# One written order for every engine, from the first load to the last store

## The chip, the cores and the metric

The kernel runs on one core of a Trainium2 chip. The metric is the device time of one execution in microseconds; smaller is better. The engines are named as in the profile: PE (TensorE, matmuls and transposes), DVE (VectorE), ACT (ScalarE), POOL (GpSimd) and SP (SyncE, which issues most DMAs). Each engine runs its own instructions strictly in the order of its queue. An instruction whose data are not there holds up everything behind it on the same engine.

## The reference

What is computed, cut to what matters (float32 in and out):

```python
# q, k, v: (4 batches, 8 heads, 768 tokens, 64)
gamma = 1.0 - 2.0 ** (-5.0 - np.arange(H))
for t in range(S):                       # retention, a state of 64 x 64 per head
    state = gamma * state + einsum('bhd,bhe->bhde', k[:, :, t], v[:, :, t])
    y[:, :, t] = 1/sqrt(D) * einsum('bhd,bhde->bhe', q[:, :, t], state)
x = y, heads side by side                # (4, 768, 512)
u = x + real(fft(fft(x, axis=1), axis=2))
un = (u - mean(u)) / sqrt(var(u) + 1e-6)
out = u + maximum(un @ w_ch1, 0) @ w_ch2     # 512 -> 2048 -> 512
```

## The kernel before, in words

**Work per batch.** A batch passes through five stages. In the attention stage the eight heads go in four pairs, numbered 0 to 3. Each pair has one load of q, one of k and one of v of 384 KB, casts to float16, transposes of q and k, scores (`wkA`) with a mask (`atm`), the chunk states (matmul `wkK`, decay into `s`) and the output (`wkY`, from the scores and from the states), which is scaled into `x`. The folding stage uses the symmetry of the transforms (`xab`, `eo`, `g`). The mixing stage makes the two transforms as matmuls (`ps`, `pq`), adds the residual (`u`) and normalizes it (`bst`, `un`). Then `un` is transposed to `unT`, by PE or by a DMA on SP. The MLP has a first product (`psh`, then relu into `ht`) and a second (`psc`, then `ob` and the store). The last batch uses seven products on sums of blocks in place of eight for its MLP (`hsum`, `wsum`). The MLP is most of PE's work, and the other stages of batch b+1 are woven into the MLP of batch b.

**What sets the order.** In the first batch, up to its first MLP matmuls, the order is written out: the strings FIRST and SECOND name one unit of work after another, and after each unit `pin()` chains the new instructions of every engine to the last one of the same engine, so that the scheduler cannot move them. The twelve loads of the first batch and the eight maskp constants are issued outside of these strings. The rest comes from `emit`: the units of a batch are put into streams, each with a first and a last due time as a fraction of a batch (DM0, TS0, DA0, LD0, MIX3, WS and others), all units are sorted by due time, and the Tile scheduler gives the order from there. `emit` pins POOL alone during batch 0 and every engine during the last batch; between them the scheduler is free. A unit there often has instructions of several engines: `a_unit`, for one, holds the score matmuls on PE and the mask product on DVE, and `ch_unit` the second product on PE, the addition on DVE and the store on SP.

**Names that the text uses.** A unit's name has its kind and then its pair or block. In the first batch `v30` and `v31` are the two halves of the cast of pair 3's v (on POOL and on ACT, L194 and L193), `v20` the cast of pair 2's v on ACT, `kv3` the state products of pair 3 (L516), `sc3` the scan behind them (L525), `am30` and `am31` score products, `yi20`, `yi21` and `yx2` the output products of pair 2 (L538, L548), `stx01` a small transpose, `x20`, `x21`, `x30`, `x31` the scaling into x (L193), `co4` a cosine table on ACT (L367), `s1m1` a part of the first transform (L782). `h00` to `h23` are the first MLP products of the first batch (L1135), `h00` the first of them and `h13` the one that the loads of batch 1 wait for. `w10` to `w13` and `w20` to `w23` are the loads of quarters of the two weights (L1311, L1318), 512 KB each, issued by POOL on a queue of its own, while all other loads go through SP.

In before POOL issues the weights in the order w10 w11 w12, v30's cast, w13, w20 to w23. The loads of batch 1 wait for the seventh weight and for `h13`:

```python
for x in (w_dma[after].ins, lb[0]["mm"].ins):
    tc.add_manual_dep(dma.ins, x.name, ...)      # after = 6
```

Of the kernel before, what the change touches and what calls it, by code (L numbers as in the profile page):

```python
# [11 lines left out]
AF = mybir.ActivationFunctionType  # L12
# [6 lines left out]
P = 128  # L19
# [13 lines left out]
DM0, DM1 = (0.120, 0.208, 0.265, 0.344), (0.004, 0.137, 0.232, 0.341)  # L33
TS0 = (0.249, 0.368, 0.406, 0.410, 0.479, 0.544, 0.680, 0.685)
TS1 = (-0.040, -0.020, 0.048, 0.585)
DA0, DA1 = (0.068, 0.080, 0.173, 0.203, 0.292, 0.326), (0.063, 0.067, 0.063, 0.158, 0.168, 0.189)
LD0, LD1 = (0.172, 0.226), (-0.370, 0.140)
HT0 = (0.655, 0.675, 0.673, 0.628)
NPE = 2
LOADS = "q0 k0 v0 q1 k1 v1 q2 k2 q3 k3 v2 v3"  # L40
# [9 lines left out]
FIRST = """  # L50
par qz0 hid hid5 gk3 q0 nid0 ta0 gk1 ta1 gk0 tq0 nid1 gk2 tn0 k00 eq0 tb0 si0 k01 v00 tk0 tn1 ab0
ek00 tb1 co0 ta3 q1 am01 tn3 ab1 am00 tb3 si1 ae000 si3 ta2 ab3 ae010 kv0 co1 ae011 yi00 tn2 sc0
co3 tb2 ab2 tq1 ae001 k10 si2 eq1 k11 co2 nsp tk1 ek10 yi01 v10 yx0 q2 am10 x01 kv1 ae100 am11 x00
sc1 tq2 k20 k21 q3 ae111 eq2 tk2 ae110 tq3 ek20 k30 ae101 am20 am21 ae200 w10 ae201 k31 ae211 yi10
yi11 ae210 yx1 tk3 w11 x10 ek30 eq3 ek31 ta4 w12 tn4 x11 am30 v30 tb4 am31 v20 ae300 stx01 fs0a
w13 si4 f512 kv2 fs0b ab4 yi20 ae301 yi21 co4 cdh0 sc2 v31 s1s10 w20 ae310 yx2 kv3 ae311 x20 s1s00
w21 sc3 x21 yi30 w22 fla yi31 yx3 flb cdh1 x31 w23 fd0 x30 xn1 f512 s1m0 fhb xn0 xm1 stx3 px1 fha
gc00a g0a fd1 s1s11 qe1 xm0 gr0 s1s01 xm2 s1m1 gc11b gc01a xmb gc11a stg00 xe gc01b gc10a stx4 gr3
stg01 g0b gr2 s21 g0c stg10 mu1 qn1 mu2 s22 ul1 stg11 qn2 uu1 stx2 ul2 ste1 gr1 un1 ste0 uu2 xl2
s23 qz1 s20 xu2 qn3 s25 ul3 qn0  # L60
"""
EARLY = (1,)
SECOND = """
h00 un2 ul0 xl3 uu0 xl0 ut1 uu3 h01 xu0 qn5 uu5 s24 xu3 ul5 h10 qn4 un3 xu5 h11 ul4 xl5 uu4 xl4
h12 xu4 ut2 h03 un4 h13 h22 h21 h23 h20 h02
"""
MIX3 = ((0.005, 0.085, 0.110, 0.125, 0.150), (0.190, 0.290, 0.310, 0.325, 0.350),
        (0.345, 0.415, 0.435, 0.460, 0.500))
WS = (0.6, 0.97)
H3_ACT = (0, 1, 2, 3, 5, 6, 7)  # L70
PROD = ((1, 4, 5, 2, 6, 7, 3), (1, 4, 6, 7, 5, 2, 3))
HS_AT = {3: (0, 4), 7: (4, 8)}
# [4 lines left out]
def kernel(  # L77
# [76 lines left out]
    def behind():  # L154
        for x in tc.nc.cur_bb.bb.instructions[mark[0]:]:
            if str(x.engine) in base:
                tc.add_manual_dep(x, base[str(x.engine)],
                                  mybir.DependencyInfo(mybir.DependencyClass.NoSync,
                                                       mybir.DependencyReason.DATA),
                                  reason="behind the first batch")  # L160

    def held(unit):
        def run():
            ins = tc.nc.cur_bb.bb.instructions
            n0 = len(ins)
            unit()
            for n in range(n0, len(ins)):
                m = n - 1
                while m >= 0 and ins[m].engine != ins[n].engine:
                    m -= 1  # L170
                if m >= 0:
                    tc.add_manual_dep(ins[n], ins[m].name,
                                      mybir.DependencyInfo(mybir.DependencyClass.NoSync,
                                                           mybir.DependencyReason.DATA),
                                      reason="casts in turn")
        return run

# [23 lines left out]
    def load_unit(b, i, after=None, names="qkv"):  # L201
        def run():
            h0 = 2 * PAIR_ORDER[i]
            for name in names:
                src = srcs[name]
                t = inp.tile([P, 2, NCH, D], f32, tag="in32", name=f"{name}32")
                rows = "h (p c) d -> p h c d" if b < NPE and name == "q" else \
                    "h (c p) d -> p h c d"
                dma = nc.sync.dma_start(t, src[b, h0:h0 + 2].rearrange(rows, p=P))
                if after is not None:  # L210
                    for x in (w_dma[after].ins, lb[0]["mm"].ins):
                        tc.add_manual_dep(dma.ins, x.name,
                                          mybir.DependencyInfo(mybir.DependencyClass.Sync,
                                                               mybir.DependencyReason.DATA),
                                          reason="loads in turn")
                if b > 1:
                    tc.add_manual_dep(dma.ins, a_of[b - 1, 1].ins.name,
                                      mybir.DependencyInfo(mybir.DependencyClass.Sync,
                                                           mybir.DependencyReason.DATA),
                                      reason="loads behind the transposes")  # L220
                in_of[name, b, i] = t
        return run

    for n in LOADS.split():
        load_unit(0, int(n[1]), names=n[0])()
# [59 lines left out]
    def late_consts():  # L285
        with tc.issue_after(lb[0]["una"].ins):
            for h in range(H):
                nc.scalar.activation(maskp[:, h // 2, h % 2], maskf, AF.Copy, bias=0.0,
                                     scale=float(gam[h] ** (-P)))
# [17 lines left out]
    def pad_unit():  # L307
        for j in range(2):
            nc.vector.memset(qzs[j][:, 0, :, D:P], 0.0)
            nc.vector.memset(qzs[j][:, 1, :, 0:D], 0.0)  # L310

    def qt_zeros():
        for j in range(2):
            nc.vector.memset(qts[j][0:D, 1], 0.0)
            nc.vector.memset(qts[j][D:P, 0], 0.0)
# [85 lines left out]
    def cast_unit(b, i):  # L401
        def run():
            h0 = 2 * PAIR_ORDER[i]
            q32, k32, v32 = (in_of.pop((n, b, i)) for n in "qkv")
            kd = kp.tile([P, NCH, 2, D], f16, tag="kd16", name="kd16")
            v16 = vp.tile([P, NCH, 2, D], f16, tag="v16", name="v16")
            with ExitStack() as es:
                if b < NPE:
                    if (b, i - 1) in last_cast:
                        es.enter_context(tc.issue_after(last_cast[b, i - 1].ins))  # L410
                    q16 = qzs[i % 2].rearrange("p h c d -> p (h c d)")[
                        :, 0:NCH * P].rearrange("p (c h d) -> p c h d", c=NCH, h=2)
                    es.enter_context(tc.issue_after(nc.gpsimd.tensor_scalar(
                        out=q16, in0=q32.rearrange("p h c d -> p c h d"), scalar1=1.0,
                        scalar2=1.0, op0=ALU.mult, op1=ALU.mult).ins))
                else:
                    q16 = qzs[i % 2]
                    for h2 in range(2):
                        dst = q16[:, h2, :, D * h2:D * h2 + D]
                        nc.gpsimd.tensor_scalar(out=dst, in0=q32[:, h2], scalar1=1.0,  # L420
                                                scalar2=1.0, op0=ALU.mult, op1=ALU.mult)
                for h2 in range(2):
                    kc = nc.gpsimd.tensor_scalar(out=kd[:, :, h2, :], in0=k32[:, h2],  # L423
                                                 scalar1=gkd[:, h0 + h2:h0 + h2 + 1],
                                                 scalar2=1.0, op0=ALU.mult, op1=ALU.mult)
                    if b < NPE:
                        es.enter_context(tc.issue_after(kc.ins))
                last_cast[b, i] = nc.gpsimd.tensor_scalar(
                    out=v16, in0=v32.rearrange("p h c d -> p c h d"), scalar1=1.0, scalar2=1.0,
                    op0=ALU.mult, op1=ALU.mult)  # L430
            q16_of[b, i], kd_of[b, i], v16_of[b, i] = q16, kd, v16
        return run
# [26 lines left out]
    def t0_unit(i, part):  # L459
        def run():  # L460
            if (0, i) not in at:
                at[0, i] = dict(kT=tp.tile([P, NCH, P], f16, tag="kT", name="kT"),
                                qT=qts[i % 2][:, 0])
# [6 lines left out]

    def te_unit(i, part, n=0):
        def run():
            st = at[0, i]
            tq = st["tq", part]
            if part == 0:
                scaled(on[f"eq{i}"], st["qT"].rearrange("p c t -> p (c t)").rearrange(
# [1052 lines left out]
```

## Time and profile before

| | us |
|---|---|
| median of 3 runs (lowest, highest) | 242.58 (242.52, 244.07) |
| the profiled execution: its span, first to last instruction | 240.1 |
| PE busy | 231.2 |
| DVE busy | 189.3 |
| ACT busy | 122.2 |
| POOL busy | 89.9 |

The median of the runs is 2.4 us above the span of the profiled execution; no other time of that execution is shown. Spans on the timeline count from the start of the profiled execution. A row of the timeline has the start, the length, the engine, the line, the operation, output and inputs with their shapes, how many instructions the row joins, and in brackets how long the engine sat idle before it and what ended that. PEld is TensorE's loading of weights, SPq the issuing of a DMA by SyncE. In the rows of DMA queues, q1 is the queue of SP's loads, stores and transposes, q0 that of POOL's weights.

### The profile page before, as it was taken

How to read it: one execution, taken by the hardware profiler on the slowest of the kernel's cores; microseconds unless marked ns; L12 is line 12 of the kernel's file. 1: busy time of each engine (PE TensorE's matmuls, PEld its weight loads, DVE VectorE, ACT ScalarE, POOL GpSimd, SP SyncE). 2: the span in 40 equal slices, each digit the busy share in tenths (PEclk: the TensorE clock that was granted, in tenths of full speed). 3: DMA queues.
4: the chain of work that ended last, by engine and by line, in shares of the span. 5: the costliest groups of instructions: out<-in, count | busy, mean ns of one | idle time of the engine just before them, and what ended most of it. 6: DMA issues, size and time to landing. Idle time of an engine off the chain costs nothing.

```text
span 240.1 us, 5658 instructions
## 1 busy us (share of the span) xinstructions
PE 231.2 (96%) x2161; PEld 159.3 (66%) x2161; DVE 189.3 (79%) x484; ACT 122.2 (51%) x273; POOL 89.9 (37%) x149
## 2 busy tenths in 40 slices
PE   6888899999999999999999999999999999999995
PEld 2465799765765645665567546665567458898884
DVE  7869989877897788996886778899985856777274
ACT  6777775667956345741247423741247316253330
POOL 6667746264400068690000554680000502240302
PEclk9659999999999999999999999999999999999999
DMA  8999999999899647999999558787100141131202
GB/s 175 252 267 195 207 197 201 230 274 248 217 220 215 120 109 164 210 189 144 263 271 212 108 110 227 131 110 171 64 26 0 26 131 44 25 111 25 87 3 87
DMA packets 99466, 36.41 MB, mean 152 GB/s; under 512 B 89840, under 2 KB 96624, under 8 KB 99440
## 3 DMA queue, kind: packets, MB, share of 16 engines
q1 hardware_dynamic: 95072, 31.79, 63.4%
q0 software_dynamic: 4224, 4.19, 10.8%
q8 instruction: 17, 0.28, 0.5%
q14 instruction: 9, 0.07, 0.1%
q10 hardware_dynamic: 144, 0.07, 0.1%
HBM read 27.26 MB, written 6.29 MB: 140 GB/s over the span
## 4 chain that ended last, share of the span: by engine, by line
PE 80%; DVE 6%; ACT 5%; POOL 3%; DMA 2%; issue 2%; SPq 0%; ACTq 0%; POOLq 0%
PE psc L1157 22%; PE psh L1118 19%; PE psh L1199 9%; PE psc L1270 8%; PE psh L1135 4%; PE wkA L622 3%; PE ps L760 3%; PE wkY L676 2%; DMA k<-in_k_dram 2%; PE wkY L672 1%; PE pq L952 1%; ACT qTz L584 1%; PE wkK L641 1%; PE pq L1006 1%; PE tq L468 1%
## 5 line engine op out<-in xcount | busy, mean ns | idle before, releaser
L1157 PE MATMUL psc<-w,ht 128*128 128x512 f16 x288 | 68.5, 379 | 0.0
L1118 PE MATMUL psh<-unT,w 128*128 128x384 f16 x320 | 59.5, 326 | 0.0
L989 POOL TENSOR_TENSOR u<-u,x 128x256 f32<-128x256 f32 x18 | 11.6, 645 | 99.2 <-DVE u L959 98.0
L1157 PEld LDWEIGHTS <-ht 128*128 128x128 f16 x288 | 27.3, 98 | 26.1 <-issue 0.2
L1118 PEld LDWEIGHTS <-w 128*128 128x128 f16 x320 | 29.9, 98 | 16.0 <-issue 0.6
L1122 ACT ACTIVATE ht<-psh 128x384 f16<-128x384 f32 x46 | 22.3, 489 | 23.9 <-PE psh L1118 23.8
L625 DVE TENSOR_TENSOR atm<-wkA,maskp 128x512 f16<-128x512 f32 x36 | 23.9, 685 | 0.7 <-PE wkA L622 0.7
L1199 PE MATMUL psh<-unT,w 128*128 128x256 f16 x192 | 21.5, 272 | 0.0
L1124 DVE TENSOR_SCALAR ht<-psh 128x384 f16<-128x384 f32 x34 | 18.7, 550 | 2.1 <-PE psh L1118 2.0
L1199 PEld LDWEIGHTS <-w 128*128 128x128 f16 x192 | 18.7, 98 | 2.2
L1055 DVE BATCH_NORM_STATS2 bst<-u 128x6 f32<-128x512 f32 x21 | 14.5, 691 | 6.9 <-POOL u L991 6.8
L1204 ACT ACTIVATE ht<-psh 128x512 f16<-128x512 f32 x21 | 12.5, 597 | 12.9 <-PE psh L1199 7.9
L1161 DVE SCALAR_TENSOR_TENSOR ob<-psc,stats,u 128x512 f32<-128x512 f32 x18 | 13.4, 745 | 6.9 <-PE psc L1157 6.7
L651 DVE SCALAR_TENSOR_TENSOR s<-s,gk,wkK 128x128 f16<-128x128 f16 x48 | 16.3, 339 | 1.9 <-ACT s L647 1.3
L684 ACT ACTIVATE x<-wkY,gexp 128x384 f16<-128x384 f32 x24 | 12.8, 581 | 9.7 <-PE wkY L676 9.7
L1060 ACT ACTIVATE un<-u,stats 128x512 f16<-128x512 f32 x15 | 10.8, 720 | 10.7 <-DVE stats L1056 7.7
L423 POOL TENSOR_SCALAR kd<-k,gexp 128x384 f16<-128x384 f32 x24 | 13.9, 588 | 3.1 <-DMA k<-in_k_dram 3.1
L622 PE MATMUL wkA<-qTz,kT 128*128 128x256 f16 x72 | 13.5, 272 | 0.2
L991 POOL TENSOR_TENSOR u<-u,x 128x256 f32<-128x256 f32 x18 | 11.4, 635 | 2.7 <-DVE stats L1056 1.8
L1135 PE MATMUL psh<-unT,w 128*128 128x128 f16 x192 | 11.4, 219 | 0.0
L954 ACT COPY qn<-pq 128x128 f32<-128x128 f32 x18 | 4.9, 274 | 12.4 <-PE pq L952 12.3
L622 PEld LDWEIGHTS <-kT 128*128 128x128 f16 x72 | 6.8, 98 | 6.3 <-ACT kT L589 0.4
(220 smaller groups left out, 432.0 us busy)
## 6 DMA issues: line engine op xcount, KB each, us to landing
q<-in_q_dram SPq DMA_DIRECT2D x16, 384.0 KB, 6.2
k<-in_k_dram SPq DMA_DIRECT2D x16, 384.0 KB, 5.5
v<-in_v_dram SPq DMA_DIRECT2D x16, 384.0 KB, 6.4
out_dram<-ob SPq DMA_DIRECT2D x18, 256.0 KB, 2.8
w<-in_moe_w_ch_dram POOLq DMA_DIRECT2D x8, 512.0 KB, 10.5
out_dram<-o SPq DMA_DIRECT2D x2, 512.0 KB, 2.9
out_dram<-o SPq DMA_DIRECT2D x3, 128.0 KB, 1.7
unT<-un SPq DMA_TRANSPOSE x15, 2.5
```

The source lines that it names most:

```text
L423: kc = nc.gpsimd.tensor_scalar(out=kd[:, :, h2, :], in0=k32[:, h2], scalar1=gkd[:, h0 + h2:h0 + h2 + 1], scalar2=1.0, op0=ALU.mult, op1=AL ...
L622: mm = nc.tensor.matmul(wk[:, c2], st["kT"][:, c, :], st["qT"][:, :, c, :], start=True, stop=True)
L625: nc.vector.tensor_tensor(out=st["atm"][:, 2 * part:2 * part + 2], in0=wk, in1=maskp[:, PAIR_ORDER[i]].unsqueeze(1).to_broadcast([P, 2, 2, ...
L651: nc.vector.scalar_tensor_tensor(out=s16[:, c], in0=s16[:, c - 1], scalar=gk2[:, hp:hp + 1], in1=wk[:, c - c0], op0=ALU.mult, op1=ALU.add)
L1055: nc.vector.bn_stats(bst, u[:, kb, :])
L1118: nc.tensor.matmul(psh, w116[:, cb, fb * P:(fb + 1) * P], unT[:, cb, rt * 384:(rt + 1) * 384], start=(cb == 0), stop=(cb == 3))
L1122: nc.scalar.activation(ht16[:, fb, :], psh, AF.Relu, bias=0.0, scale=-1.0)
L1124: nc.vector.tensor_scalar(out=ht16[:, fb, :], in0=psh, scalar1=-1.0, scalar2=0.0, op0=ALU.mult, op1=ALU.max)
L1135: mm = nc.tensor.matmul(psh[:, f], w116[:, cb, fb * P:(fb + 1) * P], unT[:, cb, kb * P:(kb + 1) * P], start=(cb == 0), stop=(cb == 3))
L1157: nc.tensor.matmul(psc, ht16[:, fb, rb3 * P:(rb3 + 1) * P], w216[:, fb, :], start=(fb == 0), stop=(fb == NFB - 1))
L1199: nc.tensor.matmul(psh[:, t], w116[:, cb, fb * P:(fb + 1) * P], unT[:, cb, p * 256:(p + 1) * 256], start=(cb == 0), stop=(cb == 3))
L1270: nc.tensor.matmul(ps[:, c0:c1], lh(f), rh(f)[:, c0:c1], start=first and f == 0, stop=last and f == 7, skip_group_check=True)
```

## The change

All units are split until each has instructions of one engine only: `t_unit` becomes `t_piece` (PE) and `te_piece` (ACT), `a_unit` becomes `a_piece` (PE) and `ma_piece` (DVE), `ch_unit` becomes `c_piece`, `o_piece` and `o_store`, `cast_unit` four `cast_piece`, and so on. One string ORDER of some 1,100 names then lists every piece of the kernel from the first load to the last store, and `play` runs the pieces in that order and pins every engine, SP with them, after each. A number ahead of a name is its batch (none for batch 0): `1kv0_0` is the first half of the state products of batch 1's pair 0, `1tk2` the transposes of batch 1's k of pair 2, `1ck0_0` and `1ck1_0` casts of k on POOL, `1cq_3` that of q of pair 3, `1lq3` its load, `1ut5` the DMA transpose of block 5 of un, `1h1_6` a first MLP product, `3dq3` and `3dk3` DMA transposes of q and k, `3a2_3` score products. The streams, the due times, `emit` and `held` are gone. The number of instructions of each operation is the same. The first batch's load order goes from q0 k0 v0 q1 k1 v1 q2 k2 q3 k3 v2 v3 to q0 k0 v0 k1 q1 k2 q2 v1 q3 k3 v2 v3. The weights are issued as w10 and w13 right behind the cast of v1, w11 ahead of v30, then w22, w12, w20, w21, w23.

The core of the diff:

```diff
-DM0, DM1 = (0.120, 0.208, 0.265, 0.344), (0.004, 0.137, 0.232, 0.341)
...
-LOADS = "q0 k0 v0 q1 k1 v1 q2 k2 q3 k3 v2 v3"
...
-FIRST = """
...
-sc1 tq2 k20 k21 q3 ae111 eq2 tk2 ae110 tq3 ek20 k30 ae101 am20 am21 ae200 w10 ae201 k31 ae211 yi10
-yi11 ae210 yx1 tk3 w11 x10 ek30 eq3 ek31 ta4 w12 tn4 x11 am30 v30 tb4 am31 v20 ae300 stx01 fs0a
-w13 si4 f512 kv2 fs0b ab4 yi20 ae301 yi21 co4 cdh0 sc2 v31 s1s10 w20 ae310 yx2 kv3 ae311 x20 s1s00
-w21 sc3 x21 yi30 w22 fla yi31 yx3 flb cdh1 x31 w23 fd0 x30 xn1 f512 s1m0 fhb xn0 xm1 stx3 px1 fha
...
+ORDER = """
+ta0 gk0 gk3 lq0 mp3 q0 par ta1 lk0 k00 mp1 nid0 f512 tn1 f512 gk2 tb1 si1 ab1 tn0 tb0 si0 qtz00
...
+qz0 k31 v10 ae111 ae101 mp7 kv1 lv2 yi11 sc1 am20 lv3 ae200 yi10 w10 yx1 x11 am21 w13 ae201 ae210
+q3 tq3 k30 eq3 v20 ae211 x10 tk3 ta4 ek31 v31 tn4 ek30 am31 ae310 tb4 ab4 si4 kv2 ae311 am30 w11
+v30 kv3 stx01 sc2 yi20 yi21 yx2 x20 x21 co4 ae301 yi31 w22 ae300 yi30 sc3 yx3 fs0a cdh0 fs0b s1s10
+fla flb x30 x31 xm1 g0a s1s00 fd0 fha w12 xm0 fhb fd1 xn1 g0b s1m0 s1s01 gc00a xmb xn0 s1s11 gc11b
+s1m1 g0c close gc01a mp6 w20 gr0 gc01b cdh1 gc11a gr3 w21 stx3 stg00 stx4 stg01 gc10a px1 s21
...
+h00 xu2 qn0 uu0 h01 ut1 te1 qn3 uu3 s25 ul3 h02 w23 h03 qn5 ul5 uu5 h13 1lv0 1lq0 1lk0 h11 xl2 ul0
+un2 ut2 te2 h12 qn4 uu4 ul4 xu0 mp0 h10 h23 xl0 h22 1lv1 1lq1 bn1 0p0_1 bn0 bn2 0rt0 h21 0p0_0
+1lk3 xl5 xu5 bn5 half un5 mp2 1lk1 xl3 0p1_1 xu3 bn3 1cv_0 h20 0p1_0 1ck1_0 1ck0_0 1kv0_0 1s0_0
...
-    def a_unit(b, i, part):
...
+    def a_piece(b, i, part):
         def run():
-            st = at[b, i]
-            if part == 0:
-                st["atm"] = ap_.tile([P, NCH, 2, P], f16, tag="atm", name="atm")
-            wk = ps_g.tile([P, 2, 2, P], f32, tag="g", name="wkA")
+            st = st_of(b, i)
+            wk = st["wk", part] = ps_g.tile([P, 2, 2, P], f32, tag="g", name="wkA")
             for c2 in range(2):
                 c = 2 * part + c2
                 mm = nc.tensor.matmul(wk[:, c2], st["kT"][:, c, :], st["qT"][:, :, c, :],
                                       start=True, stop=True)
-            a_of[b, i] = mm
+            if part == 2:
+                a_of[b, i] = mm
+        return run
+
+    def ma_piece(b, i, part):
+        def run():
+            st = st_of(b, i)
+            if "atm" not in st:
+                st["atm"] = ap_.tile([P, NCH, 2, P], f16, tag="atm", name="atm")
             nc.vector.tensor_tensor(
-                out=st["atm"][:, 2 * part:2 * part + 2], in0=wk,
+                out=st["atm"][:, 2 * part:2 * part + 2], in0=st["wk", part],
...
+            dma = nc.sync.dma_start(t, srcs[name][b, h0:h0 + 2].rearrange(rows, p=P))
+            if b == 1:
+                sync(dma, w_dma[6], lb[0]["mm"])
+            elif b > 1:
+                sync(dma, a_of[b - 1, 1])
...
-    def emit(streams):
...
+    def play(names):
+        for name in names:
+            units[name]()
+            pin()
+
+    units = first_units()
     pin()
...
-    emit(streams)
+    play(ORDER.split())
```

1057 lines of the change are left out of this document (497 added, 560 removed).

## The prediction

> **What bounds the kernel now.** I read the page's head and slices first, then the chain that ended last, then the busy time of three stretches.
>
> ```profile
> span 240.1 us, 5658 instructions
> ...
> PE 231.2 (96%) x2161; PEld 159.3 (66%) x2161; DVE 189.3 (79%) x484; ACT 122.2 (51%) x273; POOL 89.9 (37%) x149
> ...
> PE   6888899999999999999999999999999999999995
> ...
> PE 80%; DVE 6%; ACT 5%; POOL 3%; DMA 2%; issue 2%; SPq 0%; ACTq 0%; POOLq 0%
> ```
>
> The span is 240.1 us and the median of the runs 242.58, so 2.4 us lie outside the span; I make the sum inside it and add the result to 242.58. TensorE fills every slice but the first five and the last one, and 80% of the chain is TensorE.
>
> ```profile
> 0.00:33.60 33.60, 28.74 (x334) 19.97 (x335) 27.72 (x89) 25.12 (x56) 21.86 (x42) 0.85 1.16 217
> 33.60:237.40 203.80, 202.41 (x1829) 139.28 (x1826) 161.38 (x396) 97.11 (x218) 68.07 (x108) 1.00 0.69 141
> 237.40:240.20 2.80, 0.00 (x0) 0.00 (x0) 0.25 (x1) 0.00 (x0) 0.00 (x0) 0.89 0.36 115
> ```
>
> (Columns: stretch, its length, busy PE, PEld, DVE, ACT and POOL, granted clock, DMA share, GB/s.) The front, up to the first MLP matmul (unit h00), has a DMA share over 1 and no engine full. The middle is TensorE at full clock. The end is 2.8 us of last additions and stores.
>
> "Busy 202.41" hides small losses, since a matmul's end is modelled. Long pieces of the chain give the interval between matmuls when nothing is missing:
>
> ```profile
> 39.13 6.25 PE psh L1135 x112
> 134.19 10.36 PE psc L1157 x48
> 184.46 1.30 PE psh L1118 x8
> 197.47 6.99 PE psh L1199 x64
> ```
>
> That is 56 ns at 128 columns, 216 at 512, 163 at 384, 109 at 256. Both orders have the same matmuls from h00 on: 288x216 + 320x163 + 420x109 + 436x56, and 363 small ones that I put by their widths at 14.4 us (an estimate), together 198.9 us. Before needs 203.7, so the order's faults after h00 cost **4.8 us**. That is the most that a better order can win there. They show as many short waits, few of them large:
>
> ```profile
> 54.70 0.49 PE L578 MATMUL tq<-ident,kd 128*128 128x128 f16 x6 [0.25 <-ACT qTz L584]
> ```
> ```profile
> PE wkK L641 <- POOL v L428: 0.4, 1, 0.4
> PE ps L895 <- DVE xg L886: 0.2, 1, 0.2
> ```
>
> **The change, part by part.** No operation goes or comes; every engine's queue gets another order.
>
> *The front.* The loads go out in nearly the same order, v2 and v3 still last. The stretch from the last load to h00 now:
>
> ```profile
> 21.19 0.85 ACT L193 ACTIVATE v<-v 128x768 f16<-128x768 f32 x1
> 22.55 0.56 POOL L194 TENSOR_SCALAR v<-v 128x384 f16<-128x384 f32 x1 [1.50 <-DMA v<-in_v_dram]
> 22.62 0.51 ACT L367 ACTIVATE cd<-tmp,hpi 128x257 f16<-128x257 f32 x1
> 23.04 0.51 ACT L193 ACTIVATE v<-v 128x384 f16<-128x384 f32 x1
> 24.45 0.47 PE L516 MATMUL wkK<-v,kd 128*64 128x64 f16 x10
> 25.92 0.53 PE L548 MATMUL wkY<-s,qTz 64*128 64x64 f16 x10
> 26.49 1.05 ACT L193 ACTIVATE x<-wkY,gexp 128x384 f16<-128x384 f32 x2 [0.89 <-PE wkY L548]
> 27.57 0.63 ACT L741 ACTIVATE junk<-x 128x514 f16<-128x514 f16 x1
> 29.48 0.69 PE L782 MATMUL ps<-ssp,eo 128*128 128x193 f16 x6
> 33.61 1.06 PE L1135 MATMUL psh<-unT,w 128*128 128x128 f16 x16
> ```
>
> The written order puts kv3, which needs the last load, ahead of yi20, yi21 and yx2 of the pair before, and on ScalarE x10 between v20 and v31. Worked through: v20 to 22.04, x10 to 22.63, v31 to 23.15, kv3 to 23.65, then about 1.15 us of TensorE for stx01, yi20, yi21 and yx2 to 24.8; x20 and x21 (1.05) to 25.95, co4 (0.51, the row at 22.62) to 26.5, yi3 and yx3 to 27.0, x30 and x31 to 28.05, where before has 27.54. Then two "junk" means of 0.63 stand ahead of the first g copy, where before has one, and s1m1 waits for the bank that this copy frees: 0.25 more. h00 comes at 34.35 instead of 33.61: **+0.75**. Bounds: 0, if the chain closes up, and +2, if ScalarE, which also gets three maskp pieces early on, reaches v20 late (by its rows' sum it has 0.8 us to spare).
>
> *Weights ahead of loads.* POOL issues w10 and w13 right after the cast of v1, near 16 us by the sum of POOL's rows, and w11 ahead of v30; before, the first weight is issued at 18.59. At 17.7, when the first could move, some 150 packets of v2 and v3 are still to go on each DMA engine (an estimate: 1746 packets in 2 us, below, are 55 per engine and us, for 2.8 us more). Do the weights push in front? First the issue, the weights' time to landing and then the queue lines of three windows, 16.3:18.3, 18.3:20.3 and 21.3:21.9 (packets, MB, share of 16 engines):
>
> ```profile
> 18.59 2.46 POOL L1311 DMA_DIRECT2D w<-in_moe_w_ch_dram  x3
> ```
> ```profile
> DMA to landing us min/median/max: 6.2/10.5/16.6
> ```
> ```profile
> q1 hardware_dynamic: 1686, 0.43, 129.7%
> q8 instruction: 1, 0.02, 4.1%
> ```
> ```profile
> q1 hardware_dynamic: 1746, 0.44, 134.3%
> ```
> ```profile
> q0 software_dynamic: 109, 0.11, 113.5%
> q1 hardware_dynamic: 42, 0.01, 7.9%
> ```
>
> Up to 20.3 only loads (q1) move, 1.7 us after the weights' issue. In the third window one engine's worth of q1 is left (134.3%/16 = 8.4% is an engine that only works for q1; here 7.9%), and it runs at full rate while the weights (q0) fill the other fifteen. That engine is late by the instruction packet: 4.1% of 16 engines over 2 us is 1.3 us. So a queue with work left is drained and the weights fill in behind it. I cost the early issue at nothing: weights still start near 20.3. They land as before, the first at 18.59 + 6.2 = 24.8, the eighth (issued at 26.7) at 43.3, so one per 2.65 us; in the new order of issue w12 is fifth, at 35.4, and needed some 2.5 us behind h00, at 36.8. The other end of this term is in the rivals.
>
> [...]
>
> *Batch 1 earlier, its loads not.* The loads wait for the seventh weight and for h13, then come at the queue's rate; POOL casts them as they land:
>
> ```profile
> 40.99 0.37 SPq L209 DMA_DIRECT2D q<-in_q_dram  x1
> ```
> ```profile
> 45.54 0.83 POOL L413 TENSOR_SCALAR q16z<-q 128x768 f16<-128x768 f32 x1 [4.82 <-DMA q<-in_q_dram]
> 47.18 1.15 POOL L423 TENSOR_SCALAR kd<-k,gexp 128x384 f16<-128x384 f32 x2 [0.81 <-DMA k<-in_k_dram]
> 48.55 0.83 POOL L428 TENSOR_SCALAR v<-v 128x768 f16<-128x768 f32 x1 [0.23 <-DMA v<-in_v_dram]
> ...
> 60.23 0.83 POOL L413 TENSOR_SCALAR q16z<-q 128x768 f16<-128x768 f32 x1 [1.60 <-DMA q<-in_q_dram]
> ```
> ```profile
> 52.36 0.50 PE L578 MATMUL tq<-ident,q16z 128*128 128x128 f16 x6
> ```
>
> Before, TensorE first touches batch 1 at 52.36, when three loads are long cast. In the written order its first use is 1kv0_0, behind 200 matmuls of 56 ns, 16 of 216 and 4 of 109 after h00: 15.08 us, at 49.45 with h00 at 34.35. It needs the third load (k0): landed by 48.55, two casts 1.15, so 49.75. A wait of 0.3, and a lag of 49.75 - 33.61 - 15.08 = **1.05** whatever the front did up to then. The next such place is 1tk2, 11.23 us of TensorE later, at 61.0. Ahead of its kd casts POOL has the cast of q3, the tenth load: 60.23 + 0.83 + 1.15 = 62.2. Another 1.2, and TensorE stands in order behind it: the lag is now **2.25**. Lower end: 0.75, if these loads land a microsecond earlier; upper: 3.5, if the store put among them costs its own time.
>
> *The middle.* I added the mean durations of the rows along each chain of producers from one matmul to the next that needs it. In before 29 chains behind h00 are longer than the TensorE work written between; in the new order three, each by under 0.1 us. So of the 4.8 us nothing of that kind is left. What is left are the DMA transposes on SyncE:
>
> ```profile
> 100.75 2.66 SPq L1101 DMA_TRANSPOSE unT<-un  x2
> ```
> ```profile
> unT<-un SPq DMA_TRANSPOSE x15, 2.5
> ```
>
> Issue takes 1.3 each and landing 2.5. In the written order 1ut5 and 1ut3 are issued behind their un casts some 5 us ahead of 1h1_6, two issues and a landing: no slack. 3dk3 and 3dq3 stand as close ahead of 3a2_3. Each may cost 0 to 1; I take **0.75** for all, towards the middle. Engines hold: the 161.38 us of DVE spread over 203.8 leave it room.
>
> *Nothing:* stores as pieces of their own (SyncE waits, not an engine), the order of w2 (w20 lands sixth, at some 38, and is needed at 43.4), the end (same last products).
>
> Sum: lag at the end 2.25 + 0.75 = 3.0 against 4.8, so -1.8: **240.8 us**.
>
> **Rivals.**
> - *Weights in front.* If engines alternate, w10, w13 and w11 (2.65 us each) get in front of v3: between 5.3 us for two and 8.0 for three, I take 6.2, landing near 28.7. h00 comes at 40.55; h13 stands 5.1 us of TensorE behind it, so the batch-1 loads go out at 45.8 for 41.0, and 1tk2 at 60.23 + 4.8 + 1.98 = 67.0: lag 7.1 + 0.75 against 4.8, **245.6**, slower. It decides once v3 lands some 3 us late, at 25.5. For it: POOL issues early, and no row shows a weight ready while all engines have many load packets left. Against: the straggling engine. [...]
> - *Loads in time.* The instruction packets, 1.3 us each, may fall elsewhere; then k0 and q3 land about 1.1 earlier, the lag at 1tk2 is 1.1, and the time **239.7**. For it: the window above has one such packet in 2 us, the one behind it none.
> - *A written order that cannot bend.* Every engine stands at the first late item; the late casts of POOL and the transposes add 2.5 more over three batches: **243.3**. For it: no slack at three places; against: slack of microseconds at most others.
> - That the change doesn't reorder: excluded, the instruction queues of all five engines differ.
>
> **How the numbers follow.** Forecast 0.40, weights in front 0.15, loads in time 0.27, cannot bend 0.18. Its own range is 239.6 to 242. Leaving out the weights' rival and a tail below 238.4, the range is 238.4 to 245.0. One per cent is 2.4 us, about what a measurement of this kernel can tell from no change. Faster (below 240.2): most of "loads in time" and a third of the forecast, 0.38. Slower (above 245): most of the weights' rival, 0.14. Within: 0.48.
>
> **What would show it.** The last v cast on POOL at 22.5 (28 if the weights go first); first weights' packets near 20.3; h00 near 34.3; the first kd casts of batch 1 at 48.6 with wkK waiting for POOL; a wait of tq for POOL kd near 61; the middle from 62 to 237 with under 1.5 us of waits. I am wrong if v3 lands late, if TensorE waits for DVE or ACT all along the middle, or if the loads of batch 1 start later than 41.

## The result and the profile after

The changed kernel takes 254.37 us (median of 4 runs, 253.17 to 254.7) beside 242.55 for the kernel before in the same job: 1.0466 times as long, 95% interval 1.0424 to 1.0507. The forecast was 240.8, with a range to 245.0. It is slower, and by far more than any case of the prediction.

From the page of the profile after: the head, the busy time of PE and DVE, the slices of PE and its clock, and the chain that ended last, by engine and by line.

```profile
span 252.5 us, 5614 instructions
...
PE 230.2 (91%) x2161; PEld 160.5 (64%) x2161; DVE 195.8 (78%) x484; ACT 121.6 (48%) x273; POOL 94.6 (37%) x149
...
PE   7765089999999969999999998799999999999994
...
PEclk9995558999999999999999999999999999999999
...
PE 68%; DMA 13%; SPq 7%; DVE 6%; ACT 2%; POOL 1%; issue 1%; ACTq 0%; POOLq 0%; DVEq 0%
PE psc L1146 17%; PE psh L1106 16%; DMA v<-in_v_dram 9%; PE psh L1192 8%; PE psc L1242 7%; SPq L244 5%; PE psh L1128 4%; DMA unT<-un 3%; PE wkA L620 2%; DVE eo L722 2%; DMA qTz<-q16z 2%; PE ps L767 2%; DVE xab L712 1%; PE ps L805 1%; PE wkY L679 1%
```

PE's work is the same (230.2 us), the span is 12.4 us longer. Slice 5 of PE is empty. DMA has gone from 2% of the chain to 13%, and 9% of it, over 22 us, is one name: loads of v.

The windows of the profile after, cut at its own h00 (44.3) and last matmul, with columns as in the prediction:

```profile
0.00:44.30 44.30, 29.73 (x334) 20.99 (x335) 27.83 (x87) 25.72 (x60) 20.89 (x40) 0.77 0.99 179
44.30:249.30 205.00, 200.47 (x1829) 139.54 (x1827) 167.73 (x397) 95.86 (x213) 73.70 (x109) 1.00 0.66 137
249.30:252.50 3.20, 0.02 (x1) 0.00 (x0) 0.29 (x1) 0.00 (x0) 0.00 (x0) 1.00 0.39 124
18.50:38.90 20.40, 10.69 (x121) 8.55 (x122) 9.73 (x23) 8.08 (x19) 5.31 (x9) 0.50 0.90 138
```

The front is 44.3 us long where before has 33.6: 10.7 of the 12.4. The middle takes 205.0 for the 198.9 of matmul intervals, so it loses 6.1 where before loses 4.8: another 1.3. The end adds 0.4. (What a middle loses is reckoned so for every kernel below: from h00 to the end of the last matmul, less 198.9.)

POOL's timeline of the profile after shows what filled the front:

```profile
15.30 0.83 POOL L224 TENSOR_SCALAR v<-v 128x768 f16<-128x768 f32 x1 [0.80 <-DMA v<-in_v_dram]
16.08 1.72 POOL L1298 DMA_DIRECT2D w<-in_moe_w_ch_dram  x2
...
30.78 0.50 POOL L224 TENSOR_SCALAR v<-v 128x384 f16<-128x384 f32 x1 [10.81 <-DMA v<-in_v_dram]
```

and PE's, the state products of pair 3, which need that cast, and h00:

```profile
31.34 0.74 PE L525 MATMUL wkK<-v,kd 128*64 128x64 f16 x10 [8.38 <-POOL v L224]
...
44.34 1.95 PE L1128 MATMUL psh<-unT,w 128*128 128x128 f16 x32
```

The last load, v3, is cast at 30.78; before it was cast at 22.55. POOL waits 10.81 us for it, PE 8.38; the issue of w22, next on POOL, needs no load and still goes only behind this cast, at 31.24. The queue lines of four windows of the profile after (18:18.6, 19:19.6, 24:26 and 24:24.104; packets, MB, share) say why:

```profile
q1 hardware_dynamic: 514, 0.13, 126.3%
```
```profile
q0 software_dynamic: 112, 0.11, 115.7%
q1 hardware_dynamic: 37, 0.01, 10.2%
```
```profile
q0 software_dynamic: 313, 0.31, 90.3%
q1 hardware_dynamic: 313, 0.08, 30.5%
```
```profile
q0 software_dynamic: 16, 0.02, 92.3%
q1 hardware_dynamic: 16, 0.00, 29.8%
```

Up to 18.6 only loads move. When v2 is through on most engines, near 19, the weights (q0) have the engines almost alone for some 0.6 us. Then the two queues move packet for packet: 313 and 313 in 2 us, and 16 and 16 in 0.104 us, one of each for each of the 16 engines. A load packet is 256 B and a weight packet 1 KB, so v3 gets a fifth of the bytes. v3 is 1,536 packets, 96 on each of 16 engines; at 313/16 per 2 us they take 9.8 us, at the 1,746/16 per 2 us of the window in before 1.8. The difference, 8.0, is nearly all of the 8.2 by which the cast of v3 is late.

The waits of PE behind h00 in the profile after, by group:

```profile
PE psh L1106 <- DVE ob L1153: 2.0, 1, 2.0
PE ps L767 <- DVE ee L738: 1.5, 1, 1.5
PE ps L767 <- DVE ee L736: 0.9, 2, 0.5
```

Few long waits have taken the place of many short ones, and all three groups name DVE. (Two figures for a wait occur below: the idle time that a row shows, and the delay, which is the time from one matmul's start to the next less the interval that the prediction gives for it. The delay is some 0.1 to 0.2 us longer.)

### The profile page after: what moved, and what is told of

It is laid out like the page before. It is cut to its first block, busy times and chain, and to the rows that moved or that the text cites. A ratio compares the mean times of both kernels' runs of the same rounds, so it can differ in the third digit from the quotient of the medians.

```text
span 252.5 us, 5614 instructions
## 1 busy us (share of the span) xinstructions
PE 230.2 (91%) x2161; PEld 160.5 (64%) x2161; DVE 195.8 (78%) x484; ACT 121.6 (48%) x273; POOL 94.6 (37%) x149
## 3 DMA queue, kind: packets, MB, share of 16 engines
q0 software_dynamic: 4224, 4.19, 10.7%
## 4 chain that ended last, share of the span: by engine, by line
PE 68%; DMA 13%; SPq 7%; DVE 6%; ACT 2%; POOL 1%; issue 1%; ACTq 0%; POOLq 0%; DVEq 0%
PE psc L1146 17%; PE psh L1106 16%; DMA v<-in_v_dram 9%; PE psh L1192 8%; PE psc L1242 7%; SPq L244 5%; PE psh L1128 4%; DMA unT<-un 3%; PE wkA L620 2%; DVE eo L722 2%; DMA qTz<-q16z 2%; PE ps L767 2%; DVE xab L712 1%; PE ps L805 1%; PE wkY L679 1%
## 5 line engine op out<-in xcount | busy, mean ns | idle before, releaser
L1146 PE MATMUL psc<-w,ht 128*128 128x512 f16 x288 | 67.7, 379 | 0.0
L988 POOL TENSOR_TENSOR u<-u,x 128x256 f32<-128x256 f32 x36 | 22.4, 642 | 56.0 <-DVE u L974 48.4
L224 POOL TENSOR_SCALAR kd<-k,gexp 128x384 f16<-128x384 f32 x30 | 19.9, 669 | 21.1 <-PE psc L1146 8.7
L1192 PE MATMUL psh<-unT,w 128*128 128x256 f16 x192 | 22.3, 273 | 0.0
L224 POOL TENSOR_SCALAR v<-v 128x768 f16<-128x768 f32 (+1 forms) x15 | 12.7, 852 | 23.5 <-DMA v<-in_v_dram 21.5
L1117 DVE TENSOR_SCALAR ht<-psh 128x384 f16<-128x384 f32 x34 | 18.6, 552 | 2.5 <-PE psh L1106 2.2
L224 POOL TENSOR_SCALAR q16z<-q 128x384 f16<-128x384 f32 (+1 forms) x24 | 16.4, 690 | 11.0 <-DMA qTz<-q16z 10.3
L692 ACT ACTIVATE x<-wkY,gexp 128x384 f16<-128x384 f32 x24 | 13.7, 590 | 14.0 <-PE wkY L679 14.0
L1043 DVE BATCH_NORM_STATS2 bst<-u 128x6 f32<-128x512 f32 x24 | 16.4, 683 | 2.8 <-POOL u L988 2.8
L1055 ACT ACTIVATE un<-u,stats 128x512 f16<-128x512 f32 x15 | 10.7, 721 | 12.9 <-DVE stats L1044 6.8
L1280 POOL TENSOR_TENSOR u<-u,ws 128x256 f32<-128x256 f32 (+1 forms) x6 | 5.4, 925 | 27.1 <-DVE u L1280 15.5
L620 PE MATMUL wkA<-qTz,kT 128*128 128x256 f16 x72 | 12.1, 272 | 0.0
```

The source lines that it names most:

```text
L224: return (nc.gpsimd if e == "P" else nc.vector).tensor_scalar(out=out, in0=in_, scalar1=scale, scalar2=1.0, op0=ALU.mult, op1=ALU.mult)
L620: mm = nc.tensor.matmul(wk[:, c2], st["kT"][:, c, :], st["qT"][:, :, c, :], start=True, stop=True)
L988: nc.gpsimd.tensor_tensor(out=u[:, lo:hi], in0=u[:, lo:hi], in1=x[:, 1, 257:1:-1] if n else x[:, 0, 1:257], op=ALU.add)
L1043: nc.vector.bn_stats(bst, lb[b]["u"][:, kb, :])
L1117: nc.vector.tensor_scalar(out=ht16[:, fb, :], in0=psh, scalar1=-1.0, scalar2=0.0, op0=ALU.mult, op1=ALU.max)
L1146: nc.tensor.matmul(lb[b]["psc", rb], ht16[:, fb, rb % 3 * P:rb % 3 * P + P], w216[:, fb, :], start=(fb == 0), stop=(fb == NFB - 1))
```

## The experiments

### Where the weights are issued

**Weights behind the last cast of v.** The edit, in the written order:

```diff
-yi10 w10 yx1 x11 am21 w13 ae201
+yi10 yx1 x11 am21 ae201
...
-am30 w11 v30 kv3
+am30 v30 w10 w13 w11 kv3
```

> The changed kernel with w10, w13 and w11 issued behind the cast v30, nothing else moved. Theory (weights alternate with the last v load): v30 starts near 22.5 instead of 30.8, h00 near 34.3 instead of 44.3, and some 10 us go: 244 us (242.5 to 245.5). Rival (the last load is late for another reason, such as the new order of the loads): v30 stays near 30 and the time near 254.

249.19 us (249.09 to 250.0), 1.0276 of before (1.0237 to 1.0314). v3 is cast at 22.54 again, where the theory had it, so the new order of the loads isn't what made it late. The time is 3.7 above the expected range: the weights now come late, PE waits 2.5 for one at 40.6, h00 comes at 35.52 and the middle loses 10.7.

**Weights behind k30, as late as before issues them (18.9).**

```diff
-yi10 w10 yx1 x11 am21 w13 ae201
+yi10 yx1 x11 am21 ae201
...
-k30 eq3
+k30 w10 w13 eq3
```

> The changed kernel with w10 and w13 issued behind the cast k30, near 18.7 us, so that they are ready only when each engine has begun the last load. Theory A (an engine finishes the transfer that it has begun; only the next one alternates with the other queue): v30 at 22.5, the time as with the weights behind v30, within 0.7 us. Theory B (packets alternate whenever both queues have some): the engine that an instruction packet has made late alternates over its last 85 packets, v30 near 29 to 30, 252 to 254 us.

246.28 us (245.28 to 246.6), 1.015 (1.0111 to 1.019). The cast of v3 and h00 in its timelines of POOL and PE:

```profile
22.64 0.50 POOL L224 TENSOR_SCALAR v<-v 128x384 f16<-128x384 f32 x1 [1.28 <-DMA v<-in_v_dram]
```
```profile
34.04 1.95 PE L1128 MATMUL psh<-unT,w 128*128 128x128 f16 x32
```

The place of two DMA issues is worth some 8 us of the loss. The cast of v3 came as theory A had it and not as theory B; the time is 2.9 below that of the kernel with the weights behind v30, which theory A had put within 0.7. The middle loses 8.1 us here, so the rest of the order has its own price.

**The kernel before, with its weights early.** If it is the issue and not the order, before must suffer too:

```diff
-sc1 tq2 k20 k21 q3
+sc1 tq2 k20 k21 w10 w11 w12 q3
```

(`w10`, `w11` and `w12` go from their old places.)

> The kernel before with one thing moved: w10, w11 and w12 issued right behind the cast k21, near 16 us instead of 18.6. Theory (weights alternate with the last load): v30 at 28 to 31 instead of 22.55, 250 to 254 us. Rival (the rest of the written order of the changed kernel is needed for the loss): the old order has other work for TensorE while v3 is late, under 246 us.

Three executions took 249.6 to 250.9, one 245.84, so no ratio is given. POOL's timeline of the profiled one, and h00 on PE:

```profile
15.87 2.46 POOL L1311 DMA_DIRECT2D w<-in_moe_w_ch_dram  x3
...
30.66 0.51 POOL L194 TENSOR_SCALAR v<-v 128x384 f16<-128x384 f32 x1 [10.90 <-DMA v<-in_v_dram]
```
```profile
40.91 1.05 PE L1135 MATMUL psh<-unT,w 128*128 128x128 f16 x16
```

The same 8.1 us on v3 in a kernel without the written order.

**Idle matmuls ahead of kv3**, meant to keep PE's clock up (0.50 from 18.5 to 38.9 in the kernel after) while it waits: 40 products of 512 columns that nobody reads.

```diff
-v30 kv3
+v30 f512 f512 f512 f512 f512
...
+f512 f512 f512 kv3
```

> The changed kernel with 40 idle matmuls of 512 columns ahead of kv3, in TensorE's wait of 8.4 us. Theory (the wait also costs the granted clock, 0.5 until 39 us): the clock is back at 1.0 by 31, the transforms behind kv3 run at full rate, h00 near 42.6 instead of 44.3, 252.6 us. Rival (ACT and DVE set the pace behind the wait): no gain, 254 us.

250.6 us (249.86 to 253.56), 1.0358 (1.0288 to 1.0428). It didn't test the clock. POOL came to w10 0.7 us later than in the kernel after, at 16.79, v3 was not late (cast at 22.78), and the fillers stood in the way of h00 (41.82). But it showed that the loss hangs on a fraction of a microsecond. The next runs look for that edge.

**One place later on POOL**, behind the next cast:

```diff
-yi10 w10 yx1 x11 am21 w13 ae201
+yi10 yx1 x11 am21 ae201
...
-q3 tq3
+q3 w10 w13 tq3
```

> The kernel after, with the first two weights (w10, w13) one place later on POOL: behind the cast q3 instead of ahead of it, so that w10 is issued near 16.95 us and not at 16.08. Theory (an engine that has begun the last load v3 finishes it before it looks at the other queue; only an engine that finds weights ready when v2 ends alternates): the weights become ready 2.5 us behind the issue, near 19.4, when all engines have begun v3, so v3 lands near 22.6, h00 comes at 34 to 36 and the time is that of the kernel with the weights behind k30, 246.3 (245.5 to 248). Rival (weights issued ahead of the end of the loads always slow them): v3 lands 27 to 30 and the time is 251 to 254.

245.24 us (244.29 to 245.8), 1.0105 (1.0056 to 1.0155): **9.1 us less than the kernel after for one place on one queue.** Its timeline of POOL, and its load queue in the window 18.3:20.3:

```profile
17.37 1.72 POOL L1298 DMA_DIRECT2D w<-in_moe_w_ch_dram  x2
...
22.81 0.50 POOL L224 TENSOR_SCALAR v<-v 128x384 f16<-128x384 f32 x1 [2.36 <-DMA v<-in_v_dram]
```
```profile
q1 hardware_dynamic: 1748, 0.44, 133.8%
```

The window has 1,748 load packets and no weight, where before has 1,746. h00 on its PE:

```profile
36.39 0.78 PE L1128 MATMUL psh<-unT,w 128*128 128x128 f16 x11
```

From the cast 13.6, as in the kernel after; the section on the clock comes back to it. Its last matmul ends at 240.7, so the middle loses 5.4. Behind the front this kernel and the one with the weights behind k30 have the same order, and there the middle loses 8.1 with h00 2.35 earlier; the last matmuls end within 0.4 of each other (240.7 and 241.1). So the loss of a middle is no fixed price of its order: it shrinks when h00 comes late, and two kernels are best compared by it when their h00 are close.

**One weight, and two, ahead of v3.** The others go behind v30:

```diff
-am21 w13 ae201
+am21 ae201
...
-w11 v30 kv3
+v30 w13 w11 kv3
```
```diff
-w11 v30 kv3
+v30 w11 kv3
```

> The kernel after, with only w10 ahead of the last load; w13 and w11 are issued behind the cast v30. Theory (packet by packet alternation while both queues have work): an engine carries 96 packets of v3 and 32 of one weight, a weight packet takes 96 ns, so one weight costs v3 at most 32 x 96 ns = 3.1 us. Fifteen engines are through v3 near 21.6 without weights, so v3 lands near 24.6 (22.6 to 25.6), h00 comes at 36 to 38. Rival (once the weights are in front, the loads only get a fixed small share until the weights' queue is empty, or v3 has been lost behind the whole queue): v3 lands at 28 or later. The time, 248 to 251 by the theory, also holds the price of the weights behind v30 (2.6 us of waiting for a weight in the kernel with all weights behind v30).

> The kernel after, with w10 and w13 ahead of the last load and w11 behind the cast v30. Theory: two weights are 64 packets per engine, 6.1 us, so v3 lands near 27.7 (26.5 to 28.5), between one weight (24.6) and the three of the kernel after (30.7), and h00 comes at 39 to 41; time 250 to 252.5. Rival (a fixed price): v3 lands at 30 to 31 with two weights as with three.

One weight: 248.67 us (247.19 to 249.89), 1.0248 (1.0188 to 1.0308). Two: 246.25 (244.36 to 250.96), 1.0131 (1.0037 to 1.0224). POOL's timeline of each:

```profile
16.53 0.94 POOL L1298 DMA_DIRECT2D w<-in_moe_w_ch_dram  x1
...
24.46 0.51 POOL L224 TENSOR_SCALAR v<-v 128x384 f16<-128x384 f32 x1 [5.55 <-DMA v<-in_v_dram]
```
```profile
16.87 1.72 POOL L1298 DMA_DIRECT2D w<-in_moe_w_ch_dram  x2
...
22.80 0.51 POOL L224 TENSOR_SCALAR v<-v 128x384 f16<-128x384 f32 x1 [2.79 <-DMA v<-in_v_dram]
```

With one weight v3 landed at 24.39 (24.6 expected, 28 or later by the rival): one weight in front costs far less than three, as a price by what is queued in front has it. The second kernel didn't test its theory in the profiled execution: POOL reached w10 only at 16.87, and v3 wasn't late. Only its slowest execution, at 250.96, lies where two weights in front were expected, and of that there is no trace.

The traces of eight kernels by the time at which POOL issues the first weight. The fourth column counts the load packets that had still to go when the first weight packet went, divided by the 16 engines; v3 alone has 96 on each.

| kernel | first weight issued | its first packet | load packets left, per engine | cast of v3 |
|---|---|---|---|---|
| before, weights early | 15.87 | 18.43 | 121 | 30.66 |
| after | 16.08 | 18.63 | 113 | 30.78 |
| one weight ahead of v3 | 16.53 | 19.80 | 47 | 24.46 |
| idle matmuls | 16.79 | 20.46 | 14 | 22.78 |
| two weights ahead of v3 | 16.87 | 20.51 | 15 | 22.80 |
| one place later | 17.37 | 20.35 | 21 | 22.81 |
| before | 18.59 | 20.31 | 16 | 22.55 |
| weights behind k30 | 18.91 | 20.64 | 9 | 22.64 |

The upper three are late, the lower five are not. The row with one weight is the one to look at. Its queue lines from 19.8 to 24.1, the landing of v3:

```profile
q0 software_dynamic: 520, 0.52, 71.0%
q1 hardware_dynamic: 770, 0.19, 31.4%
```

Of the 770 load packets 754 are of 256 B, half of the 1,536 of v3, the last load; the other 16 are of 4 B. So v3 was half through when the weights came, and it was held up all the same.

### What the rest of the order costs

The next kernels all start from the one with the weights behind k30.

**Casts of batch 2 on POOL in the order in which their loads land** (eleven pieces; two of the places):

```diff
-1s0_2 2ck1_1 1s1_2
+1s0_2 2cv_0 2cq0_1 2cq1_1 2ck0_0 2ck1_0 1s1_2
...
-0h1_5 2cv_0 0r1_5
+0h1_5 2ck1_1 2ck0_1 0r1_5
```

The reason for it is in the timelines of the kernel that it starts from. There `2ck1_1`, whose load is the fifth, stands first, POOL waits 7.91 us for it, and its casts then fall on DVE's folds. DVE of before, then DVE and POOL of the kernel with the weights behind k30:

```profile
70.18 1.03 DVE L703 TENSOR_TENSOR xab<-x 128x780 f16<-128x780 f16 x2
```
```profile
73.94 1.64 DVE L712 TENSOR_TENSOR xab<-x 128x780 f16<-128x780 f16 x2
...
77.84 2.10 DVE L722 TENSOR_TENSOR eo<-xab 128x768 f16<-128x768 f16 x3
```
```profile
73.80 0.59 POOL L224 TENSOR_SCALAR kd<-k,gexp 128x384 f16<-128x384 f32 x1 [7.91 <-DMA k<-in_k_dram]
...
77.03 2.50 POOL L224 TENSOR_SCALAR kd<-k,gexp 128x384 f16<-128x384 f32 x2
```

Two folds take 1.64 instead of 1.03, and two casts of k 2.50 instead of the 1.15 that the prediction's row has for them: side by side, both are slower.

> The kernel with w10 and w13 behind k30, and the eleven casts of batch 2's first pairs on POOL put into the order in which their loads land, so that seven of them run in the 8 us in which POOL waits for the fifth load, ahead of DVE's folds of batch 1. Theory (POOL casts and DVE float16 folds slow each other: two xab take 1.64 us instead of 1.03, two kd 2.50 instead of 1.15, and TensorE waits 2.8 us): xab x2 back near 1.05, the wait under 1 us, 243.5 to 244.5 us. Rival (the folds are late for the data of x): rows and wait as they are, 246.3 us.

243.91 us (242.47 to 246.01, 10 runs), 1.0049 (1.0017 to 1.0081). The delays for `ee` near 81 fall from 2.04 and 0.73 to 0.11 and 0.21. The row of the first two folds did not come back as the theory had it, since a cast of v now falls on them:

```profile
75.43 1.67 DVE L712 TENSOR_TENSOR xab<-x 128x780 f16<-128x780 f16 x2
```

The second of the two takes 1.18 beside that cast. Later folds of the same stretch that stand beside no cast take 0.55, and one beside a cast of k takes 0.86. The eight folds and the `xg` behind them last from 75.43 to 80.42 here, 4.99 us, and from 73.94 to 80.64 before, 6.70 us. The middle loses 3.7. h00 is at 36.40, so the kernel to set beside it is the one with one place later (36.39): it loses 5.4 and waits 1.65 and 0.37 for `ee`, so a late h00 alone doesn't take these waits away.

**Two loads on SyncE behind the transposes they stood ahead of:**

```diff
-2y1_3 3lk3 2x1_3
+2y1_3 2x1_3
...
-1h1_0 3lk2 1h1_3
+1h1_0 1h1_3
...
-3dq1 3cq1_3
+3dq1 3lk3 3lk2 3cq1_3
```

In the kernel with the weights behind k30, PE's longest wait is at 150.9. Followed back: PE waits for `u` on DVE, DVE for POOL, POOL for a transpose of q, and that stands on SyncE behind two loads, whose issue takes 4.48:

```profile
126.95 4.48 SPq L244 DMA_DIRECT2D k<-in_k_dram  x2
131.54 2.11 SPq L587 DMA_TRANSPOSE kT<-kd  x1
133.76 1.43 SPq L583 DMA_TRANSPOSE qTz<-q16z  x1
```
```profile
137.79 0.98 POOL L224 TENSOR_SCALAR q16z<-q 128x384 f16<-128x384 f32 x2 [9.98 <-DMA qTz<-q16z]
```
```profile
150.90 0.81 PE L1106 MATMUL psh<-unT,w 128*128 128x384 f16 x4 [2.18 <-DVE u L974]
```

> The kernel with w10 and w13 behind k30, and two loads of batch 3 (3lk3, 3lk2) issued behind the DMA transposes 3dk0 and 3dq1 instead of ahead of them. Theory (SyncE stands for 4.5 us in the issue of the loads, so the transposes, POOL's q cast behind them, the additions of u and DVE's row statistics come late and TensorE waits 2.3 us near 151): that wait goes, 243.7 to 244.3 us. Rival (DVE is overloaded there in any case): the wait stays above 1.5 us, 245.5 or more.

246.18 us (245.51 to 246.66), 1.0142 (1.0102 to 1.0182). The wait at 150.9 is gone, as the theory had it, but the time is the same, as the rival had it. PE's timeline has two waits for transposes 30 us ahead of it, where the kernel that it starts from has one, of 0.60:

```profile
119.99 0.60 PE L620 MATMUL wkA<-qTz,kT 128*128 128x256 f16 x4 [0.45 <-DMA qTz<-q16z]
...
121.52 0.82 PE L1106 MATMUL psh<-unT,w 128*128 128x384 f16 x4 [0.82 <-DMA unT<-un]
...
150.43 0.81 PE L1106 MATMUL psh<-unT,w 128*128 128x384 f16 x4
```

The middle loses 5.8 instead of 8.1, and h00 came 1.9 later at a lower clock (below). The late h00 isn't what took the wait away: with one place later h00 is as late, the two loads stand where they were, and PE still sits idle for 1.60 at this matmul (150.52). But that kernel's middle loses 5.4, so the 5.8 is no gain beside it.

**Both, with two loads more moved:**

```diff
-1lv0 1lq0 1lk0
+1lv0 1lk0 1lq0
...
-1bn5 3lq0 2a2_2
+1bn5 2a2_2
...
-1ut3 3cv_0
+1ut3 3lq0 3cv_0
```

> Both of these, and 1lk0 loaded ahead of 1lq0 (0.8 us of wait at the first products of batch 1) and 3lq0 issued behind 1ut3 (0.8 us of wait for a DMA transpose). Theory (the waits add up): 246.3 - 2.2 - 2.3 - 0.8 - 0.8 = 240.2, below the kernel before (242.2). Rival (one wait hides behind another): 242 to 243.5.

242.93 us (242.37 to 244.87, 12 runs), 1.0021 (0.9995 to 1.0048). The middle loses 4.7, as in before. With h00 at 33.90 against 34.04, both at full clock, this kernel and the one that it starts from compare directly: the middle loses 3.4 less, and the time is 3.4 shorter. The theory, by which all the waits add up, had 6.1; the time is in the rival's range. New waits again: a delay of 1.8 at 125.3 and, at 61.6, the wait that the prediction put there:

```profile
61.60 0.51 PE L596 MATMUL tq<-ident,kd 128*128 128x128 f16 x6 [1.26 <-POOL kd L224]
```

**The same without 3lq0, and the cast of q3 behind the two of k that PE needs first** (`1cq_3` behind `1ck1_2`); then the same with 3lq0 and `3cq0_0` moved as well.

```diff
-1eq0_2 1cq_3 1ck0_2
+1eq0_2 1ck0_2
...
-1ck1_2 1tk2
+1ck1_2 1cq_3 1tk2
```

> The kernel with w10 and w13 behind k30, the batch-2 casts in landing order, 3lk3 and 3lk2 behind the transposes, 1lk0 ahead of 1lq0, and the cast 1cq_3 (of the tenth load of batch 1) put behind 1ck0_2 and 1ck1_2 (of the ninth). Theory (each wait that the earlier runs showed is a POOL or SyncE queue standing at a late load): the waits at 61.6 (1.4 us) and 125 (1.8) of the run before go, 239.7 us, faster than the kernel before. Rival (TensorE waits as long somewhere else): 241.5 to 242.5.

> The same with 3lq0 behind the DMA transpose 1ut3, and POOL's cast of it behind 3ck0_0. Theory: the wait of up to 0.8 us for 1ut3 near 118 goes and nothing stands behind the later load: 239.2 us. Rival (the wait for kd near 125 comes back with the later load): 241.

242.12 us (241.13 to 243.17), 0.998 (0.996 to 1.0001); and 242.23 (241.08 to 243.16), 0.9984 (0.9963 to 1.0005). PE's waits in the first, all that are listed behind h00, and its window of the middle:

```profile
PE psh L1106 <- DVE u L974: 0.8, 1, 0.8
PE ps L767 <- DVE ee L736: 0.4, 1, 0.4
```
```profile
34.90:236.20 201.30, 200.02 (x1829) 139.55 (x1827) 165.49 (x398) 95.58 (x213) 71.18 (x109) 1.00 0.71 142
```

The middle now loses 201.3 - 198.9 = 2.4 us where before loses 4.8. h00 comes at 34.94, 1.3 later than before's, and takes half of that back. Both theories had promised 2 us or more below these times (239.7 and 239.2); the first kernel came out in its rival's range, the second above its own. No version was found that is clearly faster than before.

### PE's clock in the front

With v3 cast at nearly the same time, h00 comes between 33.9 and 36.6, by the clock that PE was granted. Windows 22.5:34 of the seventh kernel (both moves and two loads) and of the last reordered one:

```profile
22.50:34.00 11.50, 10.13 (x146) 9.01 (x146) 9.54 (x28) 8.06 (x24) 5.61 (x9) 1.00 1.23 202
```
```profile
22.50:34.00 11.50, 10.84 (x132) 9.25 (x129) 8.35 (x23) 7.31 (x20) 5.56 (x9) 0.60 1.23 202
```

From the cast to h00: 11.40 at 1.00 (22.50 to 33.90) and 13.82 at 0.60 (22.73 to 36.55). The kernel with the weights behind k30 takes 11.40 at 1.00, the kernel after 13.56, of which 8.4 at 0.50. The longer the half clock behind 22.5, the later h00: none gives 33.9 and 34.0, 3.4 us give 34.9 (the first reordered kernel), 6.8 give 35.5 to 36.0 (three kernels), and some 9 give 36.4 to 36.6 (three more). What sets the half clock was not found: it came in stretches that differed from kernel to kernel, and before has it too, earlier (0.50 from 7.46 to 17.7), where it costs little: most of its own runs have spans of 240.2 to 240.6 at a mean clock of 0.98, and of 239.8 to 241.4 at 1.00.

## Why the prediction was wrong, step by step

The sum was 13.6 us too low. 9.1 of it is the weights' place (254.37 against 245.24). The other 4.4 show in the profile of the kernel with one place later: 2.0 in the front (h00 at 36.39 for 34.35, part of it at half clock) and 3.1 in the middle (5.4 lost behind h00, where the forecast's lag of 3.0 holds 0.75 of the front and so 2.25 behind it), less what the end and the time outside of the span take back. The prediction's first sign, the last v cast at 22.5 or at 28, came at 30.78.

**"A queue with work left is drained and the weights fill in behind it. I cost the early issue at nothing."** This is the step that failed. In the kernel after the weights were issued at 16.08, and their first packets went at 18.63, before v3 had begun; from then on they first had the engines almost alone and then took turns with v3, packet for packet, and v3 landed 8.2 us late. The windows of before could not show this. By its first weight packet, at 20.31, only 16 load packets per engine were left, and the one engine that was late was in the middle of v3, so they show what happens at the end of the last load, not ahead of it.

What decides when the weights get their turn stays open. The lower rows of the table look as if a load that has begun is finished first. The kernel with one weight in front contradicts that as a rule: there v3 was half through and was held up. The issue of v3 by SyncE, which ends at 17.1 to 17.3 in all of these kernels (14.64 + 2.41 in before, 14.81 + 2.40 in the kernel after), may be what counts: the weights that delayed v3 were issued 0.7 us or more ahead of its end, those that didn't 0.5 us ahead or later. No run moved that issue alone.

That the engines alternate, the condition of the first rival, shows in none of the windows of before in the prediction. The kernel after shows it: 313 packets of each queue in 2 us, and 16 of each in 0.104 us.

**The rival "weights in front"** had the mechanism, and each of its sizes was too small, 8.8 us in all. v3 landed at 30.7, not 28.7: three weights in front cost the whole 8 us. From there to h00 the kernel after took 13.65 and not 11.85, 8.4 of it at half clock, so h00 came at 44.34 for 40.55, 3.8 later. And behind h00 the rival lost 0.9 (its 7.1 + 0.75, less the 6.94 by which its h00 is late), where the kernel after lost 6.1: 5.2 more. "Against: the straggling engine" held its chance at 0.15.

**The front, +0.75.** Right in kind, too large: at full clock 11.40 from the cast to h00 beside 11.06 before, +0.34. Nothing in the step looked at the clock.

**Lag of 1.05 at 1kv0_0.** Right where it was predicted: with the weights behind k30 the delay is 0.82, the matmul comes at 49.92 and the lag is 49.92 - 33.61 - 15.08 = 1.23. In the kernel after h00 is so late that the loads are in time.

**Another 1.2 at 1tk2.** Not there with the weights behind k30 (0.12), there in the kernel with both moves (PE idle 1.26, of a delay of 1.43), where nothing ahead of it held PE up. Right as a place; hidden by waits ahead of it otherwise.

**Transposes, 0.75.** With the weights behind k30, a delay of 0.77 at 119.82 for unT. Right; in the kernel after 0.21.

**"Of the 4.8 us nothing of that kind is left"** and "DVE leaves it room". Wrong, and the second step that failed. The chains were added up with mean durations from before, where POOL is idle while DVE folds (20.98 us, up to 84.98). In the new order POOL casts at that time and both slow down: a delay of 2.8 us at `ee` with the weights behind k30, 2.25 in the kernel after. The casts in landing order took nearly all of it away. How the two engines slow each other was not found: a fold grew by 0.3 (0.86 for 0.55) beside casts that last 0.5 or more by themselves, so it doesn't wait for a whole cast.

**"Nothing: stores as pieces of their own (SyncE waits, not an engine)".** The stores did no harm that a run shows, but the loads among SyncE's transposes did: 2.3 at 150.9 with the weights behind k30. This is the rival "cannot bend" at work, by the mechanism it named: POOL and SyncE, each pinned, stood at one late item. It put 2.5 on top of the forecast's lag; behind h00 the kernels without late weights lost 5.4 (one place later) and 8.1 (behind k30) where the forecast had 2.25, so 3.1 and 5.9 on top, the slow folds included.

## What to carry to other kernels

When a second DMA queue gets work while the last needed load is still waiting or under way, that load can fall to packet-by-packet turns with it: here v3 was cast 8.2 us late behind three weights, and 1.9 behind one. Issue the bulk transfer late enough that it isn't held up, and leave a microsecond of margin, since the moment of issue itself moves: kernels with the same order up to w10 issued it at 16.08, 16.53, 16.79 and 16.87. A window in which a load wins is no rule: ask first at which point of the load it was taken. An order written for all engines is as good as its durations: price POOL and DVE work that will newly stand side by side above the mean of a profile in which they were apart (here 1.64 for 1.03 and 2.50 for 1.15). Mending one wait of a pinned order showed the next one here (61.6 and 125.3 with both moves), and a late start of the middle hid some of them (5.4 lost with h00 at 36.39, 8.1 with 34.04); compare two orders by the end of the last matmul, or by the loss of the whole middle where both start it at the same time.

## What the runs showed of the hardware

- Between weights issued at 16.53, which delayed v3, and at 16.79, which did not, lie under 0.3 us; with three weights in front v3 was cast up to 8.2 us late, with one 1.9.
- From its issue to its first packet the first weight took 1.7 us (before) to 3.7 (idle matmuls). With one weight ahead of v3, weights came in between the packets of a load that was half through (754 of 1,536 left).
- Load packets of 256 B and weight packets of 1 KB went one for one (313 and 313 in 2 us, 16 and 16 in 0.104 us), so the queue with the small packets got a fifth of the bytes.
- DVE's float16 additions and POOL's casts slowed each other side by side: an addition took 0.86 for 0.55, two casts of k 2.50 for 1.15.
- A stretch of half clock in the front moved h00 by up to 2.4 us between kernels with the same loads (13.82 from the cast for 11.40); its cause stays open. In the profiled executions the half clock of the front lasted 3.4 us behind 22.5 in the first reordered kernel, 6.8 in the one with two weights, 10.2 in before, 17.0 with one weight and 20.5 in the kernel after, each close to a multiple of 3.4.
